# Local and global attention with an FFN behind it: two block pairs at once in the first FFN product, and work moved between VectorE, GpSimd and ScalarE

## The chip, the cores and the metric

The kernel runs on one core of a Trainium2 chip. The metric is the device time of one execution in microseconds (us); the times given are medians of several runs, and a separate profiled execution of the same program supplies the trace. The engines are named as in the profile: PE (TensorE, matrix products; PEld are its weight loads), DVE (VectorE), ACT (ScalarE), POOL (GpSimd, which also issues most loads) and SP (SyncE, which issues the stores). Each engine works through its own instruction queue in the order in which it was written; semaphores hold an instruction back until what it needs is there.

## The reference

```python
# 8 batches, 8 heads, 512 local rows, 32 global rows, head size 64
s_g  = scale * q_g @ concat(k_g, k_l).T          # global rows see everything
out_g = softmax(s_g) @ concat(v_g, v_l)
s_ll = where(|pos_q - pos_k| <= 32, scale * q_l @ k_l.T, -1e9)
s_l  = concat(scale * q_l @ k_g.T, s_ll)         # local rows: 32 neighbours each way, and the global rows
out_l = softmax(s_l) @ concat(v_g, v_l)
x = concat(out_g, out_l) with heads side by side  # 8 * 544 rows of 512
h = x @ w_in                                      # 512 -> 2048
g = h * sigmoid(1.702 * h)
out = g @ w_out                                   # 2048 -> 512
```

## The kernel before

The order of all instructions is written out by hand; pools only hand out buffers. The work goes batch by batch. For a batch, the eight heads are two *quads* of four (class `Wide`), called `a` and `c` for the batch whose attention is being finished, and `a2`, `c2` for the batch after that. A quad goes through these steps:

- `Tk`, `Tq` (L509, L522): DVE transposes the loaded keys and queries. `kcopy`, `qcopy` (L503, L506) and `ext` (L528) put copies of key columns, query columns and the global queries and keys beside them.
- `S(0)`, `S(1)` (L548): PE makes the scores in two rounds, into a pair of double PSUM banks (`spair`). `X(0)`, `X(1)` (L568): ACT takes the exponential of each round in two instructions. `M(0)`, `M(1)` (L573): one product with the band mask, in place, 128 x 1760 and 128 x 1712 elements of bf16.
- `UG` (L601): PE multiplies with ones and values (`U(0)`, `U(1)`, `U(2)`, into PSUM banks `ov`) and makes the rows of the global queries (`Gm`, bank `og`). `R` (L460): DVE turns the row sums, takes reciprocals and turns them back. `XL(0)`, `XL(1)` (L470): DVE scales into `xL`, the FFN's input. `G` (L473): DVE scales the global rows straight from the bank `og` and puts them into `xG`, which is used only at the end.

The FFN of batch `i` has two parts.

- `h_some(i)` (L1165, batches 3 to 7) is the first product: 16 chunks `fc` of 128 columns of `w_in`. `h_step` (L642) takes four products of 128x512 and one ACT instruction (the activation, into `gT`). Chunks 2 and 3 instead go through `HPair(i, 1)` (L677), a pair of chunks multiplied as 2x2 blocks with seven block products in place of eight: 14 products of 128x256. It uses sums of blocks of the input (`x_sums`, L664: three of 128x512 elements named `d`, then one of 128x1024 named `s`) and of the weights (`h_weight_sums`, L656). Its steps: products 3 and 4 into PSUM tile `x`; `m3` (ACT copies out the first half of `x`); `z` (DVE adds the other half); products 1 and 6 into `y`; `zm`; products 5 and 2 into `x` again; `sub`; `inner` (ACT); product 7; `add`; `outer` (ACT).
- `phase_o(i)` (L1094) is the second product, done the same way in two row halves `p0` and `p1` (class `Pair`, L775), from sums over `gT` that DVE makes (`g_sums(i, lo, hi, which)`, L754: four sums of `hi - lo` blocks; kinds 0, 1, 3 are 256 wide and kind 2 is 512 wide per block; product 1 takes kind 0, product 6 kind 1, products 5 and 2 kind 2, product 7 kind 3). In between, it finishes the attention of batch `i+1` and begins that of batch `i+2`. At the end of `p1`, DVE runs `x_sums(i+1)`, then `sub` (L822); `evict` (ACT, L817, L113) comes after that `sub`, then the load of the activation table (`gelu_table`), and then, in `h_some(i+1)`, `m3`.

The banks: `pbank` rotates over four PSUM banks shared by `ov`, `og`, `px`, `py` and `hp`; the third chunk `hp` of `h_some` reuses the bank of `p1`'s `px`, which `sub` and `evict` read last. A batch takes 31.3 us: 17.6 in `phase_o`, 13.7 in `h_some`.

POOL before: in `phase_o(i)`, `M(0)` of `a2`, then nine issues of value loads (`load_v(i+3)`, L91) and the two issues of queries and keys; in `h_some`, the copies of `c` and `a2`. `M(1)` of `a2` is on DVE, after `p1.add`.

Code of the two products that the prediction follows, in `phase_o`:

```python
x_sums(i + 1)
if a2:
    a2.S(1)
    a2.X(1)
p1.mm(5, 2)
p1.sub()
p1.evict()
gelu_table()
p1.mm(7)
p1.add()
if a2:
    a2.M(1)
```

Of the kernel before, what the change touches and what calls it, by code (L numbers as in the profile page):

```python
# [12 lines left out]
F32 = mybir.dt.float32  # L13
BF16 = mybir.dt.bfloat16
# [6 lines left out]
def kernel(  # L21
# [12 lines left out]
    nc = tc.nc  # L34

    B, H, Sl, D = q_l.shape
# [23 lines left out]
    att = ctx.enter_context(tc.tile_pool(name="att", bufs=2))  # L60
# [27 lines left out]
    def v_view(b, n):  # L88
        return vtiles[b % 2][:, : 8 * n * (D + 2)].rearrange("p (u j c d) -> p u j c d", u=2, j=4, c=n)

    def load_v(b, hs=slice(0, 8)):  # L91
        if b == 2:
            nc.gpsimd.memset(v_view(b, 5)[:, :, :, :, D:], 1.0)
        vt = v_view(b, 5).rearrange("p u j c d -> p (u j) c d")
        vs, vg = (x[b].rearrange("h s d -> s h d") for x in (v_l, v_g))
        for c in range(5):
            n = 128 if c == 2 else 96
            nc.gpsimd.dma_start(out=vt[0:n, hs, c, :D], in_=vs[FIRST[c] : FIRST[c] + n, hs])  # L98
            if c != 2 and b != 1:
                nc.gpsimd.dma_start(out=vt[96:128, :, c, :D], in_=vg)  # L100
# [11 lines left out]
    def on_act(out_, in_):  # L112
        nc.scalar.activation(out_, in_, AF.Copy)  # L113
# [30 lines left out]
    early = ld.tile([128, 4, TB], F32, name="early", bufs=1)  # L144
# [131 lines left out]
    xG_by_row = xG.rearrange("p k (a s f) -> p k a s f", a=2, f=4)  # L276
# [223 lines left out]
    class Wide(Quad):  # L500
# [100 lines left out]
        def UG(self):  # L601
            for unit in range(3):
                self.U(unit)
            self.Gm()

    gTs, ops = {}, {}
    HT = TB // 2
    HM = d_model // 2
# [26 lines left out]
    def exp_table():  # L635
        nc.scalar.activation(spot[:, 0:1], spot[:, 1:2], AF.Exp)
# [5 lines left out]
    def h_step(i, fc):  # L642
        if fc == 0:
            gTs[i] = (moe.tile([128, FC, TB], BF16, name="gT") if i < B else
                      early.bitcast(BF16).rearrange("p a b -> p (a b)").rearrange("p (f t) -> p f t", f=FC))
        hp = pbank("hp")
        h_mm(i, fc, hp, range(NKC))
        h_act(i, fc, hp)

    w_h = {g: [w_in_c[:, g // 2, 2 * k : 2 * k + 2, g % 2, :, e] for e in range(2) for k in range(2)]  # L650
           for g in (1, 4)}
    w_s = early.bitcast(BF16).rearrange("p a b -> p (a b)")[:, : 5 * 2 * 256].rearrange(
        "p (k u c m) -> p k u c m", k=5, u=2, c=2)
    wh = {g: [w_s[:, k, u] for k in range(5)] for u, g in enumerate(w_h)}

    def h_weight_sums(g):  # L656
        w11, w12, w21, w22 = w_h[g]
        for t, x, y, op in zip(wh[g], (w11, w21, w11, w21, w12), (w22, w22, w12, w11, w22),
                               (ALU.add, ALU.add, ALU.add, ALU.subtract, ALU.subtract)):
            nc.vector.tensor_tensor(t, x, y, op)  # L660
# [93 lines left out]
    def g_sums(i, lo, hi, which=(0, 1, 2, 3)):  # L754
        n = width(i)
        if i not in sums:
            if i < B:
                sums[i] = [moe.tile([128, FC // 2, w * HT], BF16, name="gs%d" % k)
                           for k, w in enumerate((1, 1, 2, 1))]
            else:  # L760
                room = [ld.tile([128, 2, 16 * D], BF16, name=x).rearrange("p a b -> p (a b)")
                        for x in ("rk", "rq", "rk")]
                sums[i] = [x.rearrange("p (g t) -> p g t", g=FC // 2)
                           for x in (room[0][:, :1024], room[0][:, 1024:], room[1], room[2][:, :1024])]
        a11, a12, a21, a22 = parts_of(i)
        t = gTs[i].rearrange("p (g e) t -> p g e t", e=2)
        g = slice(lo, hi)
        for k in which:
            if k == 2:
                nc.vector.tensor_tensor(sums[i][2][:, g, :n], t[:, g, 0, :n], t[:, g, 1, :n], ALU.add)  # L770
            else:
                x, y, op = {0: (a11, a22, ALU.add), 1: (a21, a11, ALU.subtract), 3: (a12, a22, ALU.subtract)}[k]
                nc.vector.tensor_tensor(sums[i][k][:, g, : n // 2], x[:, g], y[:, g], op)  # L773
# [75 lines left out]
    a, c = Quad(0), Quad(1)  # L849
# [81 lines left out]
    for fc in range(4, FC):  # L931
        h_step(0, fc)
        if fc == 4:
            h_weight_sums(1)
        if fc == 12:
            h_weight_sums(4)

    def osteps(i, *sts):
# [99 lines left out]
    def loads_after(i):  # L1038
        if i + 2 < B:
            load_v(i + 2)  # L1040
        if i == 1:
            load_g(8, NQ)
        if i + 3 < B:
            load(i + 3)
# [49 lines left out]
    def phase_o(i):  # L1094
        b = i + 1
        a, c = nq[b]
        a2, c2 = quads_of(b + 1)
        p0, p1 = Pair(i, 0), Pair(i, 1)
        exp_table()
        a.UG()  # L1100
        c.S(0)
        a.R()
        g_sums(i, 7, 8, (0,))
        a.XL(0)
        g_sums(i, 7, 8, (1, 2))
        a.XL(1)
        g_sums(i, 7, 8, (3,))
        p0.mm(3, 4, 1)
        c.X(0)
        p0.m3()  # L1110
        p0.z()
        a.G()
        c.M(0)
        c.S(1)
        c.X(1)
        p0.mm(6)
        p0.zm()
        c.M(1)
        p0.mm(5, 2)
        p0.sub()  # L1120
        p0.evict()
        p0.mm(7)
        p0.add()
        p0.store()
        if a2:
            c.UG()
            c.R()
            a2.S(0)
            a2.X(0)
            a2.M(0, nc.gpsimd)  # L1130
            loads_after(i + 1)
        else:
            pt = spair()
            c.U(0, bank(pt, 0))
            c.U(1, bank(pt, 2))
            c.U(2, bank(pt, 3))
            c.Gm(bank(pt, 1))
            c.R()
        c.XL(0)
        if a2:  # L1140
            c.XL(1)
            c.G()
        p1.mm(3, 4)
        p1.m3()
        p1.z()
        if not a2:
            c.XL(1)
            c.G()
        p1.mm(1, 6)
        p1.zm()  # L1150
        x_sums(i + 1)
        if a2:
            a2.S(1)
# [5 lines that stand above are left out]
        p1.mm(7)  # L1159
        p1.add()  # L1160
        if a2:
            a2.M(1)
        p1.store()

    def h_some(i):  # L1165
        c = nq[i + 1][1] if i + 1 < B else None
        a2 = quads_of(i + 2)[0] if i + 2 < B else None
        pool = nc.gpsimd.tensor_copy
        gTs[i] = moe.tile([128, FC, TB], BF16, name="gT")
        hps = [pbank("hp"), pbank("hp")]  # L1170
        for fc in range(2):
            h_mm(i, fc, hps[fc], range(NKC))
        p = HPair(i, 1)
        p.mm(3, 4)
        p.m3()
        for fc in range(2):
            h_act(i, fc, hps[fc])
        if c:
            c.Tk(False)
            c.kcopy(pool)  # L1180
        p.z()
        p.mm(1, 6)
        p.zm()
        if c:
            c.Tq(False)
            c.qcopy(pool)
            c.ext((3,), pool)
        if a2:
            a2.Tk(False)
            a2.kcopy(pool)  # L1190
        h_step(i, 4)
        if c:
            c.ext((0,), on_act)
        h_step(i, 5)
        p.mm(5, 2)
        p.sub()
        p.inner()
        p.mm(7)
        p.add()
        h_step(i, 6)  # L1200
        p.outer()
        if a2:
            a2.Tq(False)
            transpose_g(2 * i + 4, 2 * i + 6)
            a2.qcopy(pool)
            a2.ext(copy=pool)
        if c:
            g_sums(i, 0, 2)
        h_step(i, 7)
        if c:  # L1210
            c.ext((1,), on_act)
            g_sums(i, 2, 4)
            for fc in range(8, 12):
                h_step(i, fc)
                if fc == 9:
                    c.ext((2,), on_act)
            g_sums(i, 4, 6)
            h_step(i, 12)
            h_step(i, 13)
            g_sums(i, 6, 7)  # L1220
            h_step(i, 14)
            h_step(i, 15)
            return
        p = HPair(i, 4)
        p.mm(3, 4)
        p.m3()
        g_sums(i, 0, 2, (0, 1))
        p.z()
        p.mm(1, 6)
        p.zm()  # L1230
        g_sums(i, 0, 2, (2,))
        h_step(i, 10)
        h_step(i, 11)
        p.mm(5, 2)
        p.sub()
        p.inner()
        p.mm(7)
        p.add()
        g_sums(i, 0, 2, (3,))
        h_step(i, 12)  # L1240
        p.outer()
        for k in range(3):
            for lo in (2, 4):
                g_sums(i, lo, lo + 2, (k,))
        h_step(i, 13)
        h_step(i, 14)
        h_step(i, 15)
        g_sums(i, 6, 8, (0, 1, 2))
        g_sums(i, 2, 4, (3,))
        g_sums(i, 4, 6, (3,))  # L1250
        g_sums(i, 6, 8, (3,))
# [117 lines left out]
```

## Time and profile before

| | us |
|---|---|
| median of 3 runs | 285.33 (285.22 to 285.46) |
| the profiled execution | 285.7 |
| its span, first to last instruction | 284.0 |
| `phase_o(2)` | 99.67 to 117.27 |
| `h_some(3)` | 117.27 to 130.98 |
| `phase_o(3)`, `h_some(4)` | 130.98 to 148.61, to 162.32 |
| `phase_o(4)`, `h_some(5)` | 162.32 to 180.19, to 193.90 |
| `phase_o(5)`, `h_some(6)` | 193.90 to 211.50, to 225.20 |
| `phase_o(6)`, `h_some(7)` | 225.20 to 241.50, to 255.40 |

The limits of the stages are the starts of PE's first `ov` product and first `hp` product. In timelines a line gives the start, the time until the last of the merged instructions ended, the engine, the source line, the operation, the tiles, the shapes, and how many were merged; in brackets, how long the engine was idle before it and what ended that. An instruction's recorded time includes a wait for a shared resource.

### The profile page before, as it was taken

The page shows a single profiled execution, that of the slowest core. Times are in us where ns is not written, and L with a number is a line of the kernel's source. Part 1 is how long each engine was busy: PE and PEld are TensorE (multiplying, and loading weights), DVE is VectorE, ACT ScalarE, POOL GpSimd, SP SyncE. Part 2 cuts the span into 40 slices and gives each one's busy share as a digit, 9 for nine tenths or more (in the row PEclk, how much of TensorE's full clock was granted, in tenths as well). Part 3 has the DMA queues.
Part 4 walks back from the last instruction along what each step waited for, and adds up shares of the span by engine and source line. Part 5 has one row for each costly group of instructions (what it writes and reads, how often), then busy time and mean ns, then how long its engine had stood idle before and what let it go on. Part 6 is the DMA issues. An engine that isn't in the chain of part 4 may idle for free.

```text
span 284.0 us, 9001 instructions
## 1 busy us (share of the span) xinstructions
PE 277.0 (98%) x3763; PEld 182.3 (64%) x3763; DVE 228.9 (81%) x518; ACT 182.1 (64%) x299; POOL 107.1 (38%) x172
## 2 busy tenths in 40 slices
PE   7899999999999999999999999999999999999994
PEld 6454445544554488746885588647875589558884
DVE  7584458986689899999989998999988898586452
ACT  4858757577778784688457873788459761873331
POOL 8993550765946001990079302960041000000001
PEclk9999999999999999999999999999999999999999
DMA  7999995899999801795039802980022003200223
GB/s 208 159 195 210 203 162 77 148 217 144 170 165 183 151 2 48 78 177 91 14 69 163 150 5 68 84 97 3 21 58 74 2 3 76 74 3 0 58 54 112
DMA packets 59352, 28.24 MB, mean 99 GB/s; under 512 B 47472, under 2 KB 49776, under 8 KB 59312
## 3 DMA queue, kind: packets, MB, share of 16 engines
q0 software_dynamic: 51760, 17.83, 56.2%
q1 hardware_dynamic: 7120, 9.18, 11.7%
q8 instruction: 29, 0.48, 0.7%
q10 hardware_dynamic: 432, 0.66, 0.7%
q14 instruction: 11, 0.09, 0.1%
HBM read 36.31 MB, written 8.91 MB: 159 GB/s over the span
## 4 chain that ended last, share of the span: by engine, by line
PE 86%; DVE 7%; DMA 2%; issue 1%; POOL 1%; ACT 1%; DVEq 0%; POOLq 0%; ACTq 0%
PE hp L617 31%; PE px L800 12%; PE op L731 10%; PE py L800 9%; PE x L800 6%; PE s L560 5%; PE ov L586 5%; PE s L699 3%; PE s L617 3%; DMA rq<-in_q_l_dram 2%; DVE gs L773 2%; DVE gs L770 1%; DVE xL L471 1%; DVE kT L512 1%; PE og L597 1%
## 5 line engine op out<-in xcount | busy, mean ns | idle before, releaser
L617 PE MATMUL hp<-xL,w_in_sb 128*128 128x512 bf16 x432 | 97.0, 379 | 0.2 <-DVE xL L471 0.2
L617 PEld LDWEIGHTS <-w_in_sb 128*128 128x128 bf16 x528 | 51.4, 98 | 51.8 <-issue 0.4
L622 ACT ACTIVATE gT<-hp 128x512 bf16<-128x512 f32 x108 | 62.7, 600 | 17.1 <-PE hp L617 16.6
L571 ACT ACTIVATE e<-s 128x1016 bf16<-128x1016 f32 (+1 forms) x56 | 53.3, 1003 | 25.7 <-PE s L560 25.7
L800 PEld LDWEIGHTS <-gs 128*128 128x128 bf16 x480 | 46.2, 98 | 6.6
L576 POOL TENSOR_TENSOR e<-e,mask 128x1760 bf16<-128x1760 bf16 x4 | 13.3, 3320 | 70.0 <-ACT e L571 70.0
L98 POOL DMA_DIRECT2D v<-in_v_l_dram x40 | 31.1, 780 | 13.6 <-PE og L597 3.8
L773 DVE TENSOR_TENSOR gs<-gT 128x512 bf16<-128x512 bf16 (+1 forms) x87 | 31.6, 398 | 3.3 <-ACT gT L622 3.3
L800 PE MATMUL py<-wsum,gs 128*128 128x256 bf16 x240 | 30.3, 273 | 0.0
L731 PE MATMUL op<-w_out_sb,gT 128*128 128x512 bf16 x128 | 29.5, 380 | 0.0
L576 DVE TENSOR_TENSOR e<-e,mask 128x1712 bf16<-128x1712 bf16 (+1 forms) x24 | 25.2, 1049 | 3.5 <-ACT e L571 3.5
L512 DVE STREAM_TRANSPOSE kT<-rk 128x512 f32<-128x512 f32 x14 | 14.5, 1037 | 12.6 <-DMA rk<-in_k_l_dram 12.6
L833 POOL DMA_DIRECT2D out_dram<-ob x2 | 1.2, 596 | 60.5 <-ACT ob L113 60.3
L731 PEld LDWEIGHTS <-gT 128*128 128x128 bf16 x128 | 11.8, 98 | 14.0
L800 PEld LDWEIGHTS <-gT 128*128 128x128 bf16 x192 | 18.0, 98 | 3.0
L800 PE MATMUL px<-w_out_sb,gT 128*128 128x256 bf16 x160 | 19.2, 273 | 0.1
L800 PE MATMUL px<-w_out_sb,gs 128*128 128x256 bf16 x160 | 19.1, 273 | 0.0
L471 DVE TENSOR_TENSOR xL<-ov,rs 128x512 bf16<-128x512 f32 x27 | 17.9, 686 | 1.0 <-PE ov L438 0.3
L113 ACT ACTIVATE ob<-px 128x512 f32<-128x512 f32 x10 | 6.0, 599 | 19.3 <-DVE zz L822 19.3
L770 DVE TENSOR_TENSOR gs<-gT 128x1024 bf16<-128x1024 bf16 (+1 forms) x29 | 17.2, 598 | 0.0
L560 PEld LDWEIGHTS <-kT 32*128 32x128 bf16 x672 | 12.5, 93 | 6.8 <-issue 5.7
L100 POOL DMA_DIRECT2D v<-in_v_g_dram x24 | 14.0, 585 | 2.2 <-DMA rq<-in_q_l_dram 1.7
(176 smaller groups left out, 429.3 us busy)
## 6 DMA issues: line engine op xcount, KB each, us to landing
out_dram<-ob SPq DMA_DIRECT2D x128, 64.0 KB, 2.7
rq<-in_q_l_dram POOLq DMA_DIRECT2D x5, 512.0 KB, 8.2
rk<-in_k_l_dram POOLq DMA_DIRECT2D x5, 512.0 KB, 10.0
v<-in_v_l_dram POOLq DMA_DIRECT2D x24, 96.0 KB, 4.8
w_in_sb<-in_moe_w_in_dram POOLq DMA_DIRECT2D x8, 256.0 KB, 6.9
w_out_sb<-in_moe_w_out_dram POOLq DMA_DIRECT2D x4, 512.0 KB, 10.1
rk<-in_k_l_dram POOLq DMA_DIRECT2D x5, 256.0 KB, 7.8
rq<-in_q_l_dram POOLq DMA_DIRECT2D x5, 256.0 KB, 7.2
```

The source lines that it names most:

```text
L98: nc.gpsimd.dma_start(out=vt[0:n, hs, c, :D], in_=vs[FIRST[c] : FIRST[c] + n, hs])
L471: nc.vector.tensor_mul(self.x[:, 2 * self.u + h, :], self.st[1 + h], self.st["rs"])
L512: nc.vector.transpose(flat[:, 0:Sl].rearrange("p (r t) -> p t r", t=16), loaded[self.b][0][:, self.u].bitcast(F32))
L560: nc.tensor.matmul(bank(self.ps, j)[:, at : at + n], lhsT=self.k[p, KEYS[c] : KEYS[c] + 128, e], rhs=qs[p, :, :, e], start=(e == 0), stop= ...
L571: nc.scalar.activation(self.E[rnd][:, 2 * i : 2 * i + 2, :n], self.ps[i][:, :, :n], AF.Exp, scale=scale)
L576: eng.tensor_mul(e, e, mask[:, rnd : rnd + 1, :n].to_broadcast([128, 4, n]))
L617: nc.tensor.matmul(hp[:, : width(i)], lhsT=w_in_c[:, fc // 4, kc, fc % 4 // 2, :, fc % 2], rhs=(xL[i] if i < B else xG)[:, kc, :], start=( ...
L622: nc.scalar.activation(out_, in_, AF.Gelu_apprx_sigmoid)
L731: nc.tensor.matmul(op, lhsT=gTs[i][:, fc, tci * 128 : tci * 128 + 128], rhs=w_out_sb[:, fc, :], start=(first and fc == 4 * f4), stop=(fc = ...
L770: nc.vector.tensor_tensor(sums[i][2][:, g, :n], t[:, g, 0, :n], t[:, g, 1, :n], ALU.add)
L773: nc.vector.tensor_tensor(sums[i][k][:, g, : n // 2], x[:, g], y[:, g], op)
L800: nc.tensor.matmul(out_, lhsT=lv[:, g, tt * 128 : tt * 128 + 128], rhs=rv[:, g, :], start=(g == 0 and k in ((1, 3, 4, 6) if self.apart els ...
```

## The change

- `h_some(3)` to `h_some(6)`: `HPair(i, 1, 2)` takes chunks 2 to 5 in one go, so every step of the pair handles twice the columns; chunks 4 and 5 no longer go through `h_step`. Five more weight sums are made in the first stage (`h_weight_sums(2)`).
- `g_sums`: kind 2 of blocks 4 to 7 is made in `phase_o`, before the mask product of `c`, in one instruction of 128x2048; the rest is cut into blocks 0, 1 to 3 and 4 to 6.
- `M(1)` of `a2` goes to POOL. On that queue it stands behind the last value loads and ahead of `h_some`'s loads and copies.
- `load_v(i+3)`: four of its nine issues come ahead of `M(0)` on POOL's queue, five behind. The queries and keys of batch `i+3` are issued in `h_some(i)`, after `M(1)`. In `phase_o(5)` there are no loads left to issue.
- `G` becomes `keep_og` (ACT copies `og` to SBUF) and `GG` (DVE handles both quads at once, from SBUF).
- `c2.Tk`, `c2.Tq` (DVE) go from `h_some` into the preceding `phase_o`, ahead of `x_sums`. The copies of `a2` go from POOL in `h_some` to ACT in `phase_o`.

```diff
-    def load_v(b, hs=slice(0, 8)):
+    def load_v(b, hs=slice(0, 8), chunks=range(5)):
...
+    def keep_og(q, ogs):
+        on_act(ogs[:, q.u], q.st["og"][:, : D + 2])
+
+    def GG(b, ogs):
+        rg = att.tile([128, 2, 1], F32, name="rgg")
+        nc.vector.reciprocal(rg, ogs[:, :, D : D + 1])
+        xg = att.tile([128, 2, D], BF16, name="xgg")
+        nc.vector.tensor_mul(xg, ogs[:, :, :D], rg.to_broadcast([128, 2, D]))
+        for u in range(2):
+            nc.vector.transpose(xG_by_row[:, 2 * u : 2 * u + 2, b // 4, :, b % 4],
+                                xg[:, u].rearrange("p (d h) -> p h d", h=2))
...
         if fc == 12:
+            h_weight_sums(2)
             h_weight_sums(4)
...
     def phase_o(i):
+        late = a2 and i > 2
+        wide = 2 < i < B - 1
-        g_sums(i, 7, 8, (1, 2))
+        g_sums(i, 7, 8, (1,) if wide else (1, 2))
...
         p0.z()
-        a.G()
+        if wide:
+            g_sums(i, 4, 8, (2,))
+        keep_og(a, ogs)
+        if late:
+            a2.kcopy(on_act)
+            a2.qcopy(on_act)
         c.M(0)
         c.S(1)
         c.X(1)
         p0.mm(6)
         p0.zm()
         c.M(1)
+        if late:
+            a2.ext(copy=on_act)
...
             c.R()
+            keep_og(c, ogs)
+            if i + 3 < B:
+                load_v(i + 3, chunks=(0, 1))
             a2.S(0)
             a2.X(0)
             a2.M(0, nc.gpsimd)
-            loads_after(i + 1)
+            if i + 3 < B:
+                load_v(i + 3, chunks=(2, 3, 4))
...
             c.XL(1)
-            c.G()
+            GG(b, ogs)
         p1.mm(3, 4)
         p1.m3()
         p1.z()
+        if c2:
+            c2.Tk(False)
         p1.mm(1, 6)
         p1.zm()
+        if c2:
+            c2.Tq(False)
         x_sums(i + 1)
...
         if a2:
-            a2.M(1)
+            a2.M(1, nc.gpsimd)
         p1.store()
...
     def h_some(i):
-        p = HPair(i, 1)
+        gs = (1, 2) if c else (1,)
+        fcs = iter([fc for fc in range(2, 8) if fc // 2 not in gs])
+        p = HPair(i, *gs)
...
         if c:
-            c.Tk(False)
+            if i + 3 < B:
+                load(i + 3)
             c.kcopy(pool)
+            c.qcopy(pool)
+            c.ext((3,), pool)
+        if a2:
+            a2.Tk(False)
         p.z()
         p.mm(1, 6)
         p.zm()
-        if c:
-            c.Tq(False)
-            c.qcopy(pool)
-            c.ext((3,), pool)
-        if a2:
-            a2.Tk(False)
-            a2.kcopy(pool)
+        if c:
+            g_sums(i, 0, 1)
...
         p.sub()
         p.inner()
         p.mm(7)
         p.add()
...
-            a2.qcopy(pool)
-            a2.ext(copy=pool)
...
+            h_step(i, 8)
+            p.outer()
+            g_sums(i, 1, 4)
...
+            g_sums(i, 4, 7, (0, 1, 3))
```

More of the change, by code (lines that the diff above doesn't have):

```diff
@@ L95, in load_v @@
         vs, vg = (x[b].rearrange("h s d -> s h d") for x in (v_l, v_g))
-        for c in range(5):
+        for c in chunks:
             n = 128 if c == 2 else 96
@@ L650 @@
     w_h = {g: [w_in_c[:, g // 2, 2 * k : 2 * k + 2, g % 2, :, e] for e in range(2) for k in range(2)]
-           for g in (1, 4)}
-    w_s = early.bitcast(BF16).rearrange("p a b -> p (a b)")[:, : 5 * 2 * 256].rearrange(
-        "p (k u c m) -> p k u c m", k=5, u=2, c=2)
+           for g in (1, 2, 4)}
+    w_s = early.bitcast(BF16).rearrange("p a b -> p (a b)")[:, : 5 * 3 * 256].rearrange(
+        "p (k u c m) -> p k u c m", k=5, u=3, c=2)
     wh = {g: [w_s[:, k, u] for k in range(5)] for u, g in enumerate(w_h)}
@@ L1098, in phase_o @@
         p0, p1 = Pair(i, 0), Pair(i, 1)
+        ogs = att.tile([128, 2, D + 2], F32, name="ogs", bufs=1)
+        late = a2 and i > 2
         exp_table()
@@ L1138, in phase_o @@
             c.R()
+            keep_og(c, ogs)
         c.XL(0)
@@ L1145, in phase_o @@
         p1.z()
-        if not a2:
+        if c2:
+            c2.Tk(False)
+        else:
             c.XL(1)
-            c.G()
+            GG(b, ogs)
         p1.mm(1, 6)
         p1.zm()
+        if c2:
+            c2.Tq(False)
         x_sums(i + 1)
@@ L1184, in h_some @@
         if c:
-            c.Tq(False)
-            c.qcopy(pool)
-            c.ext((3,), pool)
-        if a2:
-            a2.Tk(False)
-            a2.kcopy(pool)
-        h_step(i, 4)
+            g_sums(i, 0, 1)
+        h_step(i, next(fcs))
         if c:
             c.ext((0,), on_act)
-        h_step(i, 5)
+        h_step(i, next(fcs))
         p.mm(5, 2)
@@ L1199, in h_some @@
         p.add()
-        h_step(i, 6)
-        p.outer()
         if a2:
@@ L1204, in h_some @@
             transpose_g(2 * i + 4, 2 * i + 6)
-            a2.qcopy(pool)
-            a2.ext(copy=pool)
-        if c:
-            g_sums(i, 0, 2)
-        h_step(i, 7)
-        if c:
-            c.ext((1,), on_act)
[L1212 to L1217, printed above, removed]
+        if not c:
+            h_step(i, next(fcs))
+            p.outer()
+            h_step(i, next(fcs))
+        else:
+            h_step(i, 8)
+            p.outer()
+            g_sums(i, 1, 4)
+            h_step(i, 9)
+            c.ext((1,), on_act)
+            h_step(i, 10)
+            c.ext((2,), on_act)
+            h_step(i, 11)
             h_step(i, 12)
             h_step(i, 13)
-            g_sums(i, 6, 7)
+            g_sums(i, 4, 7, (0, 1, 3))
             h_step(i, 14)
```

## The prediction

> **What bounds the kernel.** First the busy times of the page, then the busy times stage by stage (columns: stretch, its length, busy time and instructions of PE, PEld, DVE, ACT, POOL, then clock, DMA share, GB/s).
>
> ```profile
> PE 277.0 (98%) x3763; PEld 182.3 (64%) x3763; DVE 228.9 (81%) x518; ACT 182.1 (64%) x299; POOL 107.1 (38%) x172
> ```
> ```profile
> 162.32:180.19 17.87, 17.73 (x394) 15.22 (x393) 16.62 (x38) 10.85 (x14) 4.62 (x3) 1.00 0.14 35
> 193.90:211.50 17.60, 17.60 (x393) 15.16 (x393) 16.07 (x36) 10.74 (x14) 3.32 (x1) 1.00 0.13 33
> ```
>
> PE is busy without a hole in nearly every stage, at clock 1.00, so the time falls only where PE's work falls. DVE is the next engine: 16.07 of 17.60 us. Once it was too late: phase_o(4) takes 17.87 us, 0.27 more than phase_o(5). The chain of waits says why: PE waits for DVE to read the bank that the next product needs.
>
> ```profile
> 163.78 0.64 DVE sT L462
> ...
> 164.46 1.91 PE px L800 x16
> ...
> 211.66 1.73 PE hp L617 x8
> 213.39 0.87 PE s L699 x8
> 214.26 1.73 PE hp L617 x8
> 215.99 0.65 PE s L699 x6
> ```
>
> The last four lines price the pair: eight full products take 1.73 us (216 ns each), fourteen half-width ones 0.87 + 0.65 (109 ns each).
>
> Third, the timelines of DVE, POOL and ACT at the end of phase_o(5), the stage that decides.
>
> ```profile
> 206.75 0.28 DVE L478 TENSOR_SCALAR xg<-og,rg 128x64 bf16<-128x64 f32 x1
> ...
> 208.75 2.06 DVE L673 TENSOR_TENSOR sT<-xL 128x512 bf16<-128x512 bf16 x2
> 210.74 0.41 DVE L673 TENSOR_TENSOR xs<-xL 128x512 bf16<-128x512 bf16 x1
> 211.07 0.68 DVE L674 TENSOR_TENSOR rs<-xL 128x1024 bf16<-128x1024 bf16 x1
> 211.68 0.67 DVE L822 TENSOR_TENSOR zz<-zz,px 128x512 f32<-128x512 f32 x1
> ```
> ```profile
> 206.88 3.32 POOL L576 TENSOR_TENSOR e<-e,mask 128x1760 bf16<-128x1760 bf16 x1 [16.23 <-ACT e L571]
> ```
> ```profile
> 208.97 1.89 ACT L571 ACTIVATE e<-s 128x992 bf16<-128x992 f32 x2 [1.90 <-PE s L560]
> 212.44 0.60 ACT L113 ACTIVATE ob<-px 128x512 f32<-128x512 f32 x1 [1.58 <-DVE zz L822]
> ```
> ```profile
> 239.86 0.73 DVE L673 TENSOR_TENSOR sT<-xL 128x512 bf16<-128x512 bf16 x2
> ```
>
> The same two sums of x_sums take 0.73 us where POOL is idle (239.86) and 2.06 where POOL's mask product runs until 206.88 + 3.32 = 210.20. The first one stands still until then; its successor starts at 210.40. DVE sums with one operand in PSUM run through it (the `XL` products and `zm` beside this product have their usual lengths). Sums with both operands in SBUF and a POOL product over SBUF exclude each other. And who goes first when both are waiting shows in the window at 126 us:
>
> ```profile
> 126.11 0.52 DVE L773 TENSOR_TENSOR gs<-gT 128x512 bf16<-128x512 bf16 x1
> 126.29 0.50 POOL L540 COPY q<-qgT 128x144 bf16<-128x144 bf16 x1
> 126.56 0.78 DVE L770 TENSOR_TENSOR gs<-gT 128x1024 bf16<-128x1024 bf16 x1
> ```
>
> The POOL copy (0.30 us alone, at 157.34) asks during one DVE sum, gets in when that ends, and the next sum (0.68 alone, at 128.65) waits for it.
>
> **The change, part by part.**
>
> *Products.* In four stages 8 x 216 ns give way to 14 x 109 ns: 1.73 - 1.53 = 0.20 us each, **-0.80 us** in all. PE has no holes there, so this is on the path.
>
> *DVE in h_some.* Off go `Tk` (0.96), `Tq` (0.62) and kind 2 of blocks 4 to 6 (0.60 + 0.34); the doubled `z`, `zm`, `sub`, `add` add about 2 x 0.30 + 2 x 0.55. Copies leave POOL, and with them waits such as the 1.26 us of the first sum at 156.71, which alone takes 0.41. So DVE enters phase_o(4) sooner than at 163.7, and the hole goes: **-0.27**.
>
> *DVE in phase_o.* On come `Tk`, `Tq` and the 128x2048 sum (1.13, from 0.34 for 512 and 0.60 for 1024); off go `M(1)` (1.0) and the first `G` (0.68). In front of `M(0)` DVE is then 1.13 - 0.68 - 0.34 = 0.1 us later for the same start. The half `p0.add` waits for PE anyway, with about 0.1 us to spare. Cover: PE's `p0` products. If it fails, everything DVE does for `c` is that much later. Kind 2 is ready 6.15 us into the stage (`z` at 4.7, its 0.33, then 1.13), product 5 starts at 6.1 and reaches block 4 at 6.55.
>
> *ACT.* `keep_og`, `kcopy` and `qcopy` (66, 192 and 384 elements; from ACT's 72 elements at 0.15 and 256 at 0.27 between starts, together 0.85 us) fit before `X(1)` of `c`, where ACT idles 1.03 to 1.14 us. `ext` fits in the 1.7 us before `evict`. Without that cover `X(1)` would be late, and `c.M(1)` has 0.5 us until PE's `UG`. Nothing. The five weight sums (1.7 us) lie in DVE's idle 7.34 us before 32.19, which waits for a load. The loads land within 10.1 us by the page and are used a stage of 13 us or more later. Nothing.
>
> *M(1) on POOL, stages 2 to 4.* Behind `M(0)` come five issues (0.6 to 0.84 us each, 3.6 in all), so it runs from 2.4 to 5.7 us after `h_some`'s start, when `x_sums` is done. It meets the four sums of block 0, written ahead of `sub`: they wait until 5.7, `sub` (1.17 us from 0.34 and 0.61 for 256 and 512) ends at 7.8, `inner` (0.97), chunk 8 (0.5), `outer`, chunk 9 at 10.8. PE wants chunk 9's bank for chunk 13 at 10.87. Bounds per stage: 0, or 0.3 if ACT is later by that. I take **+0.1** for the three.
>
> *M(1) on POOL, phase_o(5).* No loads stand between. X(1) ends at 208.97 + 1.89 = 210.86, so `M(1)` asks at 210.94 (0.08 later, as `M(0)` after its own), during the third sum of `x_sums`, which ends about 211.1. The fourth, `s`, is due at 211.07. By the window at 126 us POOL goes first, for 3.32 x 1712/1760 = 3.2 us, to 214.3; `s` gives way to `sub` at 214.8, not 211.68. Behind `sub` stand `evict` (then 215.55, ends 216.15), the table load and `m3` (start 2.02 us after `evict`'s, ends 218.15). PE: product 6 needs `s` at 214.53, waits 0.3; the third chunk needs `px`'s bank at 215.3, waits 0.9; product 5 needs `m3` at 217.9, waits 0.25; product 2 needs `z`, 0.25; product 7 needs `zm`, 0.2. Sum **+1.9 us**. The bounds are 0 (DVE goes first, the sum takes its 0.60) and 3.0: the three copies behind `M(1)` (0.35, 0.5, 0.4) can also go ahead of `s`, as three did at 156.71.
>
> This is where the Trainium skill bears ("SBUF — State Buffer", section "Who interferes with whom"): a DVE instruction with two SBUF inputs and a GpSimd instruction that reads SBUF exclude each other, and the one that issues first holds the port for its whole length. The trace agrees: 2.06 against 0.73 us. By its issue order alone, `M(1)` at 210.94 is ahead of `s` at 211.07, and the sum comes out as here; the other order would give 284.4.
>
> **Sum:** -0.80 - 0.27 + 0.1 + 1.9 = **+0.9 us**. Against the profiled execution's 285.7 (span 284.0 and 1.7 around it) that is 286.6; against the median, 0.37 lower, **286.3**.
>
> **The rivals.**
>
> *The sum goes first (faster).* If DVE issues `s` before POOL gets in, or `X(1)` is 0.15 us later against `x_sums`, `M(1)` starts at 211.7 and delays nothing: 285.33 - 0.97 = 284.4. For it: 0.13 us decide. Against it: `M(0)` ends at 210.20 and four sums cannot be through by 210.94; at 126 us POOL got in three times running.
>
> *GG too is shut out (slower still).* `G` read PSUM; `GG`'s product has both operands in SBUF, as the sums that stood still. Its place is 206.75, and `M(0)` starts at 206.88 (with four issues ahead, 2.75 us after PE's `UG`, about 0.05 later). If DVE is over 0.12 us late there, `GG` waits until 210.2, `z` ends at 211.1, and PE's product 5 at 208.87 waits 2.2 us. One such stage gives 286.3 + 2.2 = 288.5. For it: the margin. Against it: `p0.add` is released by PE, which resets DVE to the place it had.
>
> The same page of the Trainium skill names all two-input DVE instructions, which would include `GG`'s f32 product; no row here shows one.
>
> *Nothing left (no change).* DVE's sum goes first in phase_o(5), but the meeting in `h_some` costs 0.25 us in each of four stages: 284.4 + 0.9 = 285.3. Against it: ACT caught up by chunk 12 before.
>
> **How the numbers follow.** Forecast 0.52, the sum first 0.22, GG shut out 0.15, nothing left 0.11. A measurement of this kernel tells about 0.2% (0.57 us) from no change, so faster is below 284.76 and slower above 285.90. Of the forecast's chance 0.03 falls below 285.9, of the first rival's 0.01 above 284.76: faster 0.21, same 0.15, slower 0.64. The forecast's own range is 285.8 to 287.4 (1.9 us replaced by 1.5 and 3.0). The range reaches down to the first rival and up to one stage of the second: 284.2 to 288.6.
>
> **What would show it.** Right: in phase_o(5) the fourth `x_sums` sum recorded at some 3.8 us, `evict` 3.1 us later against PE's first `hp` product, holes of 1.9 us in PE before product 6, chunk 6 and products 5, 2, 7; elsewhere h_some of 13.5 us. Wrong: the fourth sum at 0.68 there; or product 5 of `p1` waiting in several stages, with `GG`'s product at over 3 us; or h_some at 13.7 in stages 3 to 5, which would leave no saving.

## The result, and the profile after

| | before | after |
|---|---|---|
| median of 6 runs, us | 285.37 (285.12 to 285.76) | 287.56 (287.20 to 287.97) |
| ratio, 95% interval | 1 | 1.0077 (1.0064 to 1.0090) |
| profiled execution, its span | 285.7, 284.0 | 287.36, 285.6 |
| batch from `phase_o(2)`, from PE's first `ov` product to the next batch's | 31.31 | 31.11 |
| from `phase_o(3)` | 31.34 | 31.16 |
| from `phase_o(4)` | 31.58 | 31.76 |
| from `phase_o(5)` | 31.31 | 33.43 |

The changed kernel is 0.8% slower, 2.2 us. The first two batches are shorter by about the 0.20 us that the double pair was to save; the last two give back all of that and more. The busy times of the page, then those of four stretches (stretch, length, busy time and instructions of PE, PEld, DVE, ACT, POOL, clock, DMA share, GB/s):

```profile
PE 275.6 (96%) x3764; PEld 184.8 (65%) x3787; DVE 229.9 (81%) x489; ACT 186.7 (65%) x319; POOL 113.6 (40%) x158
```
```profile
161.63:179.22 17.59, 17.59 (x393) 15.14 (x394) 17.19 (x35) 12.66 (x23) 7.08 (x7) 1.00 0.35 48
179.22:193.39 14.17, 13.66 (x77) 7.34 (x76) 12.20 (x20) 10.48 (x20) 7.17 (x8) 1.00 0.57 66
193.39:210.99 17.60, 17.60 (x393) 15.16 (x394) 17.20 (x35) 12.67 (x23) 3.86 (x2) 1.00 0.14 34
210.99:226.82 15.83, 14.04 (x76) 7.31 (x75) 12.01 (x16) 10.38 (x20) 4.31 (x4) 1.00 0.14 34
```

PE's share fell from 98 to 96%. It still has no hole (time in which it is idle) in `phase_o(4)` and `phase_o(5)`, the first and third line; the holes are in `h_some(5)` (0.51 us) and `h_some(6)` (1.8). `phase_o(4)` is down from 17.87 to 17.59, so its old hole is gone. The timelines of DVE, POOL, ACT and PE at the last one:

```profile
206.23 0.29 DVE L613 TENSOR_TENSOR xgg<-ogs,rgg 128x128 bf16<-128x128 f32 x1
...
208.99 1.32 DVE L685 TENSOR_TENSOR sT<-xL 128x512 bf16<-128x512 bf16 x2
210.24 0.41 DVE L685 TENSOR_TENSOR xs<-xL 128x512 bf16<-128x512 bf16 x1
210.58 3.73 DVE L686 TENSOR_TENSOR rs<-xL 128x1024 bf16<-128x1024 bf16 x1
214.23 0.68 DVE L834 TENSOR_TENSOR zz<-zz,px 128x512 f32<-128x512 f32 x1
```
```profile
206.36 3.35 POOL L576 TENSOR_TENSOR e<-e,mask 128x1760 bf16<-128x1760 bf16 x1 [19.96 <-ACT e L571]
210.48 3.28 POOL L576 TENSOR_TENSOR e<-e,mask 128x1712 bf16<-128x1712 bf16 x1 [0.77 <-ACT e L571]
```
```profile
214.94 0.60 ACT L113 ACTIVATE ob<-px 128x512 f32<-128x512 f32 x1 [4.54 <-DVE zz L834]
```
```profile
214.36 0.60 PE L711 MATMUL s<-rs,early 128*128 128x256 bf16 x4 [0.17 <-DVE rs L686]
215.59 1.89 PE L629 MATMUL hp<-xL,w_in_sb 128*128 128x512 bf16 x8 [0.63 <-ACT ob L113]
218.31 1.03 PE L711 MATMUL s<-xL,early 128*128 128x256 bf16 x8 [0.83 <-DVE ob L719]
```

`M(1)` (210.48) asks 0.10 us before the fourth sum of `x_sums` (210.58) is due. That sum is recorded at 3.73 us instead of 0.68; `sub` (L834), `evict` (ACT) and the table load follow late; and PE waits in turn for the sum, for the bank that `evict` frees, and for `z` (L719).

### The profile page after: what moved, and what is told of

It reads as the page before. It is cut to its first block, busy times and chain, and to the rows that moved or that the text cites. A ratio compares the mean times of both kernels' runs of the same rounds, so it can differ in the third digit from the quotient of the medians.

```text
span 285.6 us, 9003 instructions
## 1 busy us (share of the span) xinstructions
PE 275.6 (96%) x3764; PEld 184.8 (65%) x3787; DVE 229.9 (81%) x489; ACT 186.7 (65%) x319; POOL 113.6 (40%) x158
## 5 line engine op out<-in xcount | busy, mean ns | idle before, releaser
L629 PE MATMUL hp<-xL,w_in_sb 128*128 128x512 bf16 x385 | 89.1, 379 | 2.0 <-ACT ob L113 0.6
L629 PEld LDWEIGHTS <-w_in_sb 128*128 128x128 bf16 x496 | 48.2, 98 | 49.8 <-issue 2.5
L634 ACT ACTIVATE gT<-hp 128x512 bf16<-128x512 f32 x100 | 56.8, 603 | 12.5 <-PE hp L629 12.0
L576 POOL TENSOR_TENSOR e<-e,mask 128x1760 bf16<-128x1760 bf16 (+1 forms) x8 | 26.4, 3302 | 20.8 <-ACT e L571 20.7
L785 DVE TENSOR_TENSOR gs<-gT 128x256 bf16<-128x256 bf16 (+2 forms) x75 | 29.8, 427 | 5.8 <-ACT gT L634 5.8
L743 PE MATMUL op<-w_out_sb,gT 128*128 128x512 bf16 x122 | 28.8, 379 | 0.5 <-issue 0.3
L576 DVE TENSOR_TENSOR e<-e,mask 128x1760 bf16<-128x1760 bf16 (+1 forms) x20 | 20.9, 1051 | 3.0 <-ACT e L571 3.0
L634 ACT ACTIVATE gT<-s 128x1024 bf16<-128x1024 f32 (+1 forms) x10 | 9.3, 937 | 13.3 <-DVE ob L725 8.8
L782 DVE TENSOR_TENSOR gs<-gT 128x1024 bf16<-128x1024 bf16 (+3 forms) x21 | 16.1, 772 | 0.0
```

The lines of the kernel that those rows point to most:

```text
L576: eng.tensor_mul(e, e, mask[:, rnd : rnd + 1, :n].to_broadcast([128, 4, n]))
L629: nc.tensor.matmul(hp[:, : width(i)], lhsT=w_in_c[:, fc // 4, kc, fc % 4 // 2, :, fc % 2], rhs=(xL[i] if i < B else xG)[:, kc, :], start=( ...
L634: nc.scalar.activation(out_, in_, AF.Gelu_apprx_sigmoid)
L743: nc.tensor.matmul(op, lhsT=gTs[i][:, fc, tci * 128 : tci * 128 + 128], rhs=w_out_sb[:, fc, :], start=(first and fc == 4 * f4), stop=(fc = ...
```

## The experiments

All are edits of the changed kernel, except the one that starts from the kernel before. Ratios are to runs of the kernel before on the same chip. The batch times are read as in the table above.

**M(1) of phase_o(5) alone back on DVE.**

```diff
-            a2.M(1, nc.gpsimd)
+            a2.M(1, nc.gpsimd if i + 3 < B else nc.vector)
```

> M(1) of phase_o(5) alone goes back to VectorE, all else as changed. Port theory (M(1) gets in ahead of the last x_sums sum, 2.1 us of holes in PE): the fourth sum is recorded at 0.68 us instead of 3.73, the holes before product 6, chunk 6 and product 5 go, the batch from phase_o(5) to phase_o(6) takes 31.1 to 31.3 us instead of 33.43, median 285.3 to 285.6. Rival, x_sums is late because Tk and Tq now stand ahead of it: the batch stays above 32.5 us, median above 287.

Measured: 285.27 us, ratio 0.9989 (0.9975 to 1.0003). The batch from `phase_o(5)` takes 31.10 us instead of 33.43. That one instruction's place costs 2.3 us, in the median as in the trace (2.5 by the ratios). The fourth sum came out at 0.88 us, not at the 0.68 that was expected: with `M(1)` gone from POOL's queue, the three copies of `c` run beside the last sums of `x_sums`. PE has no hole there.

**M(1) stays on POOL, but waits for x_sums.** A copy of two elements of the fourth sum's output stands ahead of it on POOL.

```diff
+            if i + 3 == B:
+                behind(xs["s"][0:1, 0, 0:2])
             a2.M(1, nc.gpsimd)
```

> M(1) stays on GpSimd everywhere, but in phase_o(5) it is held until the last x_sums sum has been written. Port theory: as good as taking it off GpSimd, 285.3 to 285.7, since only the order at the port matters. Rival, GpSimd's 3.3 us for M(1) are themselves too long: M(1) now ends about 1 us later, and the time stays at 287.5 or above.

Measured: 285.23 us, ratio 0.9980 (0.9966 to 0.9993), that batch 31.11 us. POOL's product is later than in the changed kernel and lasts as long, and PE has no hole behind it. The DVE and POOL timelines of this run:

```profile
210.47 0.68 DVE L686 TENSOR_TENSOR rs<-xL 128x1024 bf16<-128x1024 bf16 x1
```
```profile
211.21 0.18 POOL L642 COPY spot_p<-rs 1x2 bf16<-1x2 bf16 x1 [1.62 <-DVE rs L686]
211.35 3.23 POOL L576 TENSOR_TENSOR e<-e,mask 128x1712 bf16<-128x1712 bf16 x1
```

So POOL's speed is not the cause; the order of the two instructions is.

**The sums of block 0 behind add as well.** This builds on the first experiment.

```diff
         p.zm()
-        if c:
-            g_sums(i, 0, 1)
...
         p.add()
+        if c:
+            g_sums(i, 0, 1)
```

> M(1) of phase_o(5) on VectorE, and the four sums of block 0 in h_some moved from ahead of sub to behind add. Port theory: nothing is left between M(1) or the copies on GpSimd and sub, so the 0.67 us of holes in h_some(5) go as well: 284.6 to 284.9. Rival, those holes come from ScalarE's longer inner and outer steps: they stay, and the time equals that of the run with M(1) of phase_o(5) alone on VectorE.

Measured: **284.55 us**, ratio 0.9969 (0.9956 to 0.9982), the lowest median of all versions and faster than both kernels. All four batches take 31.09 to 31.10 us, and PE is never idle:

```profile
179.04:192.55 13.51, 13.51 (x78) 7.32 (x75) 11.30 (x21) 10.62 (x20) 6.83 (x8) 1.00 0.59 69
```

What the move removed is seen in the changed kernel's timelines of `h_some(4)` and `h_some(5)`: DVE's sums of block 0 with `sub` (L725) behind them, then POOL beside them.

```profile
153.30 0.94 DVE L785 TENSOR_TENSOR gs<-gT 128x256 bf16<-128x256 bf16 x2
154.17 0.41 DVE L782 TENSOR_TENSOR gs<-gT 128x512 bf16<-128x512 bf16 x1
154.50 0.28 DVE L785 TENSOR_TENSOR gs<-gT 128x256 bf16<-128x256 bf16 x1
154.70 1.21 DVE L725 TENSOR_TENSOR ob<-ob,s 128x1024 f32<-128x1024 f32 x1
...
184.40 1.11 DVE L785 TENSOR_TENSOR gs<-gT 128x256 bf16<-128x256 bf16 x2
185.43 0.72 DVE L782 TENSOR_TENSOR gs<-gT 128x512 bf16<-128x512 bf16 x1
186.07 0.48 DVE L785 TENSOR_TENSOR gs<-gT 128x256 bf16<-128x256 bf16 x1
186.47 1.21 DVE L725 TENSOR_TENSOR ob<-ob,s 128x1024 f32<-128x1024 f32 x1
```
```profile
150.63 3.25 POOL L576 TENSOR_TENSOR e<-e,mask 128x1712 bf16<-128x1712 bf16 x1
153.82 0.77 POOL L81 DMA_DIRECT2D rq<-in_q_l_dram  x1
...
181.75 3.26 POOL L576 TENSOR_TENSOR e<-e,mask 128x1712 bf16<-128x1712 bf16 x1
184.94 0.42 POOL L504 COPY kT<-kT 128x192 f32<-128x192 f32 x1
185.31 0.56 POOL L507 COPY qc<-q 128x384 bf16<-128x384 bf16 x1
185.82 0.58 POOL L545 COPY kT<-kgT 128x256 bf16<-128x256 bf16 x1
```

In `h_some(4)` two load issues follow `M(1)`, and DVE gets through its sums in 1.4 us. In `h_some(5)` there is nothing left to load: the three copies follow at once, take turns with the sums, and these last 2.1 us. `sub` starts 7.04 us after the first `hp` product that the trace has of the stage (179.43) instead of 6.37 (148.33), ACT's `inner` is late with it, and PE waits for a bank (0.41 us of recorded hole; the batch is 0.67 us longer than in the best version):

```profile
190.71 2.75 PE L629 MATMUL hp<-xL,w_in_sb 128*128 128x512 bf16 x12 [0.41 <-ACT gT L634]
```

This loss is apart from that of `phase_o(5)`: in the two runs with `M(1)` of `phase_o(5)` alone moved or held the batch from `phase_o(4)` still took 31.76 us. Moving the copies instead of the sums was not tried.

**M(1) on DVE in all stages.** The last argument of `a2.M(1, nc.gpsimd)` goes.

> M(1) goes back to VectorE in all stages, the rest as changed. Port theory: no long GpSimd product meets x_sums or the sums of block 0; VectorE gets 1.0 us more in each stage, where it has idled 0.9 us waiting for m3: 284.5 to 285.0. Rival, VectorE's load is what M(1) was moved for: R comes late in the next phase_o and PE waits for its banks, above 285.6.

Measured: 284.69 us, ratio 0.9973 (0.9962 to 0.9985), batches of 31.09 to 31.10 us. The two intervals overlap, so this version and the one before cannot be told apart. Moving `M(1)` to GpSimd bought nothing here: DVE has the 1.0 us for it.

**The best version with a single pair.** `gs = (1,)` in `h_some`, chunks 4 and 5 through `h_step` again.

> The best version so far (M(1) of phase_o(5) on VectorE, sums of block 0 behind add) with a single pair again in h_some. Theory: PE is packed in both, so the time rises by four times 0.20 us, to 285.3 to 285.5, each h_some at 13.71 us instead of 13.51. Rival: the moved work is what gained, and the time stays at 284.5.

Measured: 285.43 us, ratio 0.9982 (0.9967 to 0.9998). By the medians that is 0.88 us more, but the two were measured on different chips, and by their ratios to the kernel before the difference is only some 0.4 us. The trace is clearer: batches of 31.29, 31.34 and 31.30 us, 0.20 to 0.25 more each. The last took 31.52; its other 0.2 us were not followed up.

**The double pair as the only change to the kernel before.**

> The kernel before with the double pair in batches 3 to 6 as the only change (and the weight sums that it needs). Theory: PE has 0.80 us less to do, but VectorE, which filled 13.4 of 13.7 us in h_some before, gets 1.6 us more there and has to be waited for at the start of phase_o: 286.5 to 289. Rival: VectorE catches up in phase_o, where it has room, and the gain shows: 284.4 to 284.8.

Measured: 290.94 us, ratio 1.0177 (1.0149 to 1.0204), past the upper end of what was expected. The waits of PE in this run (engine, line, what it waited for: total, times, longest), then DVE at the start of `phase_o(4)`, where PE wanted the bank 1.6 us before it got it:

```profile
PE px L800 <- DVE sT L462: 5.7, 4, 1.6
```
```profile
165.64 0.41 DVE L770 TENSOR_TENSOR gs<-gT 128x512 bf16<-128x512 bf16 x1
165.97 0.28 DVE L773 TENSOR_TENSOR gs<-gT 128x256 bf16<-128x256 bf16 x1
166.18 0.70 DVE L462 STREAM_TRANSPOSE sT<-ov 128x512 f32<-128x512 f32 x1
```

It is the old hole of `phase_o(4)`, grown from a recorded 0.14 to 1.6 us and found behind all four of the changed `h_some`: DVE is still at the sums of the batch before when `R` is due. It does not catch up. So the pair pays only together with other parts of the change. The moves off DVE in `h_some` are the likely ones, but they were not tried one by one.

**The five value loads of phase_o(4) behind M(1).** This starts from the best version.

```diff
-            if i + 3 < B:
+            if i + 3 < B and i != 4:
                 load_v(i + 3, chunks=(2, 3, 4))
...
             a2.M(1, nc.gpsimd if i + 3 < B else nc.vector)
+            if i == 4:
+                load_v(i + 3, chunks=(2, 3, 4))
```

> The best version so far, with the five value loads of phase_o(4) put behind M(1) instead of between M(0) and M(1). Port theory: M(1) now asks 0.8 us after M(0) ends and shuts out the last x_sums sum as it did in phase_o(5): that sum at 3.7 us, some 2.0 us of holes in PE in h_some(5), 286.4 to 286.8. Rival, phase_o(5) was slow for a reason of its own (the last batch with two quads ahead): nothing changes, 284.5.

Measured: 286.81 us, ratio 1.0039 (1.0027 to 1.0051), 2.3 us above the best version by the medians, 2.0 by the ratios (two chips again); the batch from `phase_o(4)` takes 33.47 us. The fault of `phase_o(5)` has been made in `phase_o(4)`; DVE, then POOL:

```profile
178.80 0.41 DVE L685 TENSOR_TENSOR xs<-xL 128x512 bf16<-128x512 bf16 x1
179.14 3.73 DVE L686 TENSOR_TENSOR rs<-xL 128x1024 bf16<-128x1024 bf16 x1
```
```profile
174.91 3.34 POOL L576 TENSOR_TENSOR e<-e,mask 128x1760 bf16<-128x1760 bf16 x1
178.79 3.53 POOL L576 TENSOR_TENSOR e<-e,mask 128x1712 bf16<-128x1712 bf16 x1 [0.54 <-ACT e L571]
```

Five load issues are what keeps the two mask products apart in the earlier stages.

**GG of phase_o(3) moved into M(0).** `GG(b, ogs)` stands behind `p1.z()` for `i == 3`; best version otherwise.

> The best version so far, with GG of phase_o(3) written behind z, so that it falls into M(0) on GpSimd. Theory of the second rival: GG's f32 product has two SBUF operands and is shut out: recorded at about 3 us instead of 0.29, Tk and zm late, PE's product 7 of p1 and evict late, 1.5 to 2.5 us more. Rival: only the bf16 sums are shut out; the product takes 0.3 us and the time stays within 0.2 us.

Measured: 290.80 us, ratio 1.0173 (1.0144 to 1.0201), 6.2 us above the best version by the medians, 5.8 by the ratios, far more than expected; the batch from `phase_o(3)` takes 37.57 us. DVE, POOL, then PE:

```profile
144.68 2.98 DVE L613 TENSOR_TENSOR xgg<-ogs,rgg 128x128 bf16<-128x128 f32 x1
...
149.80 5.12 DVE L685 TENSOR_TENSOR sT<-xL 128x512 bf16<-128x512 bf16 x2
```
```profile
144.16 3.34 POOL L576 TENSOR_TENSOR e<-e,mask 128x1760 bf16<-128x1760 bf16 x1
...
151.05 3.24 POOL L576 TENSOR_TENSOR e<-e,mask 128x1712 bf16<-128x1712 bf16 x1
```
```profile
149.33 1.03 PE L812 MATMUL py<-wsum,gs 128*128 128x256 bf16 x8 [1.49 <-DVE zz L827]
...
154.98 0.73 PE L711 MATMUL s<-sT,w_in_sb 128*128 128x256 bf16 x4 [2.89 <-DVE sT L685]
155.50 1.06 PE L711 MATMUL s<-xs,w_in_sb 128*128 128x256 bf16 x4
```

`GG`'s f32 product is shut out just like the bf16 sums: 2.98 us instead of 0.29. That price was right, and so was the hole that follows from it, 1.49 us before product 7 of `p1`. But the lateness brings `x_sums` up to `M(1)`: its first sum is recorded from 149.80 and ends at 154.58, 0.29 us after `M(1)`, and PE is idle for 2.9 us more. That sum asked 1.25 us before `M(1)` is recorded to start, while POOL still issued two loads. In the trace of the changed kernel 19 bf16 sums run beside nothing but load issues on POOL, all at their usual lengths, so what held this one until 151.05 is not shown.

## Why the prediction was right, and where it was short

287.56 us lies in the range of 284.2 to 288.6, but just above the forecast's own, 285.8 to 287.4. *The mechanism and the sign* were right, and so were the place and the instruction. `s` was forecast at some 3.8 us and took 3.73; the holes in PE were forecast before product 6, chunk 6 and products 5, 2 and 7, and the trace has them before product 6, chunk 6 and product 5, where the waits for `m3` and `z` fell into one. Undoing the order by two routes removed the loss, and repeating it in another stage brought it back.

*M(1) in phase_o(5), +1.9 us*, measured 2.3 (33.43 against 31.10). The starts of PE's products, set against those of the best version, tell where the rest is: product 6 came 0.3 us later, chunk 6 a further 0.8 and product 5 a further 1.0, where the forecast had 0.3, 0.9 and, for products 5, 2 and 7 together, 0.7. Product 5 was held until `z` ended at 218.26, not only until `m3` ended at 217.54. Another 0.2 us came behind product 7 and was not followed up. The copies of `c` behind `M(1)` were named as the upper bound; here they did not get ahead of `s`, which ran as soon as `M(1)` ended at 213.76 and was through at 214.31.

*Products, -0.80 us*: confirmed by the run with a single pair, 31.29 us or more a batch against 31.10. *The old hole, -0.27*: gone from the trace, though the best version is only 0.92 us below the kernel before by their medians. How much of the hole the kernel before has in other executions was not measured; its profiled execution lies 0.37 us above the median, so the hole may be larger there than in most.

*The step that failed* is "M(1) on POOL, stages 2 to 4 ... I take +0.1 for the three". Its bound was 0.3 us per stage. The batch from `phase_o(4)`, with `h_some(5)` in it, took 31.76 us, 0.67 more than the 31.09 of the best version, and the median fell by 0.72 us when the sums of block 0 were moved. The forecast had seen that nothing is loaded in `phase_o(5)`, but not that `h_some(5)` too has no loads: the copies then follow `M(1)` directly and get in between the very sums that stand ahead of `sub`. 2.3 + 0.7 - 0.8, with nothing for the old hole, is 2.2 us, the measured change of the median; the forecast had +0.9.

*The faster rival* (the sum goes first) fell: POOL got in with 0.10 us to spare. That is little, and the forecast had said so; had `X(1)` ended 0.2 us later, this rival's order could have come out, so the outcome owes something to luck. All six executions lie between 287.20 and 287.97 us, so the order does not seem to vary from one to the next. *GG shut out* did not happen in the changed kernel: its product started at 206.23, `M(0)` at 206.36. The margin of 0.13 us was forecast as 0.12, and the experiment shows that the instruction's own price, some 3 us, was no invention; the time of that run was far above the rival's 2.2 us. Here the Trainium skill ("SBUF — State Buffer", section "Who interferes with whom") was the better guide than the trace of before: it names every DVE instruction with two SBUF inputs, and the f32 product at 2.98 us agrees. *Nothing left* fell with the first rival.

*One reading under the forecast* was off: in the trace of before the `XL` products of `phase_o(5)` do not run beside `M(0)`; they end at 206.63, ahead of its start at 206.88. What runs beside it at its usual length is `z` (207.23, 0.41 us) and `zm` (208.41, 0.42 us). The conclusion stands on these two.

*DVE in h_some*: the forecast counted the work taken off DVE there only as the 0.27 us of the old hole. The run with the pair alone, 5.2 us slower than the kernel before, shows that without the rest of the change the pair would not have paid at all.

## What to carry to other kernels

An instruction moved to an idle engine brings its resources along: list which instructions of the busy engine need the same port during its whole length, and what stands behind them in their queue. When issues or loads between two long instructions thin out towards the last batches, check the last batches by themselves; what keeps two instructions apart may be work that ends there. Before pricing a saving on the full engine, ask whether the second fullest can keep up: here it could only with other parts of the change beside it.

## What the runs showed of the hardware that was not expected

In the run with `GG` moved, PE was idle for 2.9 us at 152 to 155, longer than in any other hole here. From 155.5 on, each product of 128x256 took 213 ns instead of 109 in the trace, until 158.1. The granted clock in the stretches (columns as above) says the same; the holes of up to 0.83 us in the changed kernel left it at 1.00, and so did those of up to 1.60 us in the run with the pair alone.

```profile
150.40:155.00 4.60, 1.70 (x8) 0.61 (x8) 4.60 (x3) 0.00 (x0) 4.58 (x5) 1.00 0.90 58
155.00:158.00 3.00, 3.00 (x16) 2.21 (x17) 2.91 (x5) 1.50 (x2) 1.85 (x4) 0.56 0.70 117
158.00:161.00 3.00, 3.00 (x18) 1.67 (x16) 1.56 (x3) 2.99 (x8) 0.00 (x0) 0.88 1.08 186
```

The products from 154.98 to 160.13 take 5.15 us where 16 x 109 ns and 8 x 216 ns would make 3.47: 1.7 us of this execution went to the slower clock, so here the long hole cost more than its own length. Whether it does so each time is open: of the four executions of this run, two have a mean clock of 0.992 (291.13, the profiled one, and 291.00 us) and two have 1.000 (290.60 and 290.42). The two pairs differ by some 0.6 us, not by 1.7; no trace shows the holes of the others.
